# Listing the third chunk's output ahead of the fourth chunk's preparation, with an order edge behind it

## The chip, the cores and the metric

The kernel runs on one core of one Trainium2 chip. The metric is the device time of one execution in microseconds (us); lower is better. The engines are TensorE (PE in the profile, with PEld for its weight loads), VectorE (DVE), ScalarE (ACT), GpSimd (POOL) and SyncE (SP), which issues most of the DMA transfers.

## The reference, cut to what matters

Three layers follow each other, all in float32:

```python
# 1. linear attention with decay: batch 4, 8 heads, 768 steps, head size 48
for t in range(S):
    state = alpha[:, :, t, :, None] * state + einsum('bhd,bhe->bhde', k[:, :, t], v[:, :, t])
    y[:, :, t] = einsum('bhd,bhde->bhe', q[:, :, t], state)
# 2. dense layer over 3072 tokens, 384 -> 2048 -> 384
h = x @ w_in;  x = (h * cos(h)) @ w_out
# 3. routed experts: 8 experts, 384 -> 1024 -> 384, one expert for each token
#    with x @ w_skip > 0; the other tokens pass unchanged
out[t] = x[t] + gate[t] * (relu(x[t] @ w1[e]) @ w2[e])
```

## The kernel before, in words

**Chunks and groups.** The 3072 tokens are cut into 24 chunks of 128 steps. They are worked on in the order given by ORDER: the first chunks of three of the batches come first (indices 0, 1 and 2), then the rest; index 3 is the second chunk of the first batch. Three chunks make a group, and a group is the 384 columns that the dense layer takes at once. So the dense layer can start once the chunks 0, 1 and 2 have all delivered their columns. In this document the first chunk is index 0, the third is index 2, the fourth is index 3 and the fifth index 4.

**One chunk.** `prep(n, j)` has six parts, written p*nj* in the opening list: p*n*0 is the check of the decay's maximum (nothing for the first six chunks, whose check is `lim` on ScalarE), p*n*1 the first scan on VectorE (L401, and for the fourth chunk `lim` behind it: L378 and L380 on ScalarE), p*n*2 small operations for the seed of the second scan (L408, L411, L413), p*n*3 the second scan (L415), p*n*4 the product of q and k with the decays (L424; for the chunks 0 to 2 half of it is on GpSimd, L421), p*n*5 copies of k on ScalarE (L389), preceded for the fourth chunk by a scaling of a state on VectorE (L520). Then come T (transposes of k, L435 and L437), S0 and S1 (scores, L444 and the masked copy L445), Y0 and Y1 (the output in PSUM, L454 to L460) and U (the state, L500 and L511 to L514). a*n* is `lim` of a chunk on its own.

**The split of the output.** Y1 ends with the split of the output into a high part, rounded to the matmul's format (a copy on ScalarE), and a low part, the rest (a subtraction on VectorE), written to the tile X of the group. The first 96 rows go in one step, L480 and L481. The last 32 rows need another place: for most chunks through a small tile x3 (L475, L476) and DMAs (`s_late`, L491). For the third chunk, the only one in DIRECT, they are written to X straight from PSUM in three steps (L471 on ScalarE and L472 on VectorE, one pair for each of three blocks), and `s_late` issues nothing. Y*n*0 and Y*n*1 are called in the list as Y20 and Y21 for the third chunk.

**The weights.** w_in and w_out are stored as 64-bit numbers and come in 32 pieces. `piece64` is a generator with a step for each part of a piece: load (SP, L67), two copies on ScalarE (L76, L77), two operations on VectorE (L79, L82; the result is one of four buffers, YB), the high part on ScalarE (L309) and the low part on GpSimd (L310); a piece of w_out also goes through TensorE for the gate columns (L316 to L327). Five load buffers are used in turn (SB64). In the opening list, each g*i* is one step of the generator i; the pieces 0, 1 and 3 are of w_in, 2 and 4 of w_out.

**The dense layer.** For a slice f of 128 hidden columns `m_L1` is nine matmuls (L541), then L544 on ScalarE and L545 on VectorE; `m_mid` is the sine (L552, ScalarE) and a product (L553, VectorE); `m_split` is a copy (L560, ScalarE) and a subtraction (L562, GpSimd); `m_L2` is nine matmuls (L576). A group has 16 slices, and slice f needs piece f of both weights.

**What sets the order.** PRE is the opening list, written by hand; it is traced before the main loop's slots t = 0, 1, and so on. While it is traced, SP and GpSimd keep the written order (`manual_schedule`). TensorE, VectorE and ScalarE have a planner: it takes, by its own model of durations, the ready instruction that was traced first, so an instruction that is listed later can be issued earlier where the earlier one isn't ready. Steps that aren't in the list (the later weight pieces, the fifth chunk) are traced in the main loop. Each engine then runs its instructions in the order that came out. Loads of rows (`a_load_w`, tag w, L359) have two buffers, those of q and k (L365) three; a load waits until all readers of its buffer are done.

Of the kernel before, what the change touches and what calls it, by code (L numbers as in the profile page):

```python
# [7 lines left out]
F32 = mybir.dt.float32  # L8
# [5 lines left out]
ACTF = mybir.ActivationFunctionType  # L14
ALU = mybir.AluOpType
AX = mybir.AxisListType

B, H, S, D = 4, 8, 768, 48
# [22 lines left out]

PRE = """
w1 w0 p01 q2 q1 p11 q0 c g1 v0 w2 v1 g0 g2 g3 p02 p03 g4 p04 p12
T0 q3 mk g0 v2 p05 w3 p00 S00 p10 p20 p21 a0 a2 S01 Y00 p13 p14 Y01 p22 U0 p23 p24 p15 S10 S11 g0 g0 Y10 g2 p25 p30 g1 T1 p31 L0 U1 Y11 g1 S20 T2 S21 p32 p33 L1 Y20 g2 Y21 g3 p34 L2 g3 a1 U2 p35 g2 g3 g1
""".split()
LASTV = 1
RB = 2
# [181 lines left out]
def linear_attention_moe_kernel(outer, tc, qk, al, v, w_in, w_out, w1, w2, idw, cst, csti, fill, q0, k0, v0, alpha0, out):  # L229
    nc = tc.nc  # L230
# [144 lines left out]
    def lim(n):  # L375
        wA = raw[n][:, 8 * RL:16 * RL]
        junk = w64.tile([PR, 8 * RL], U8, tag="sq", name="sq", bufs=1)
        nc.scalar.activation(out=junk, in_=wA, func=ACTF.Relu, bias=lims[0:PR, 0:1], accum_out=amax[:, n:n + 1])  # L378
        i = NCH + LIM_ACT.index(n)
        nc.scalar.activation(out=junk, in_=wA, func=ACTF.Relu, scale=-1.0, bias=lims[0:PR, 1:2], accum_out=amax[:, i:i + 1])  # L380
# [49 lines left out]
    def s_T(n):  # L430
        if n not in NEXT:
            return
        pt = ps.tile([P, 512], F32, tag="t", name="pt")
        for p in range(NP):
            nc.tensor.transpose(pt[:, PR * p:PR * p + PR], QK[n][:, 1, p, :], ident[0:PR, 0:PR])  # L435
        t = at.tile([P, NP, PR], F32, tag="kT", name="kT", bufs=1)
        nc.scalar.activation(out=t.rearrange("p a b -> p (a b)"), in_=pt[:, 0:NP * PR], func=ACTF.Copy)  # L437
        kT[n] = t

    def s_S(n, i):  # L440
        N = 128 - 64 * i
        sc = ps.tile([P, 512], F32, tag="acc0" if i and n < 3 else "s", name="sc")[:, 0:NP * N].rearrange("p (a b) -> p a b", b=N)
        for p in range(NP):
            nc.tensor.matmul(sc[:, p, :], KB[:, 1 - i, p, :], QK[n][:, 0, p, 64 * i:128], start=True, stop=True)  # L444
        nc.vector.copy_predicated(out=scm[i], mask=mask[:, :, 0:N], data=sc)  # L445

    def s_Y(n, i):
        if i == 0:
            YP[n] = ps.tile([P, NP, 128], F32, tag="y", name="y")
        y = YP[n]  # L450
        first = FIRST[n]
        for p in (3, 0) if i == 0 else (1, 2):
            if not first:
                nc.tensor.matmul(  # L454
                    y[0:96, p, :], state(n)[:, p, :], QK[n][:, 0, p, :], start=True, stop=False, skip_group_check=True
                )
            nc.tensor.matmul(  # L457
                y[0:96, p, :], Vt[n][:, 1, p, :], scm[0][:, p, :], start=first, stop=False, skip_group_check=True
            )
            nc.tensor.matmul(  # L460
                y[0:96, p, 64:128], Vt[n][:, 2, p, :], scm[1][:, p, :], start=False, stop=True, skip_group_check=True
            )
        if i == 1:
            g, c = grp_of[n]
            if c == 0:
                X[g] = mo.tile([P, 2, 3, 128 * len(GROUPS[g])], F32R, tag="x", name="x")
            sl = slice(128 * c, 128 * c + 128)
            if n in DIRECT:
                for j in range(3):
                    hi, lo, yj = X[g][96:128, 0, j, sl], X[g][96:128, 1, j, sl], y[32 * j:32 * j + 32, 3, :]  # L470
                    nc.scalar.activation(out=hi, in_=yj, func=ACTF.Copy)  # L471
                    nc.vector.tensor_tensor(out=lo, in0=yj, in1=hi.bitcast(F32), op=ALU.subtract)  # L472
            x3 = n not in DIRECT and at.tile([96, 2, 128], F32R, tag="x3", name="x3")
            if x3:
                nc.scalar.activation(out=x3[:, 0, :], in_=y[0:96, 3, :], func=ACTF.Copy)  # L475
                nc.vector.tensor_tensor(  # L476
                    out=x3[:, 1, :], in0=y[0:96, 3, :], in1=x3[:, 0, :].bitcast(F32), op=ALU.subtract
                )
            hi, lo = X[g][0:96, 0, :, sl], X[g][0:96, 1, :, sl]
            nc.scalar.activation(out=hi, in_=y[0:96, 0:3, :], func=ACTF.Copy)  # L480
            nc.vector.tensor_tensor(out=lo, in0=y[0:96, 0:3, :], in1=hi.bitcast(F32), op=ALU.subtract)  # L481
            late[n] = x3


    def s_late(n):
# [9 lines left out]
    def s_U(n):  # L495
        if n not in NEXT:
            return
        u = ps.tile([P, 512], F32, tag="acc1" if n < 3 else "t", name="u")[:, 0:8 * D].rearrange("p (a b) -> p a b", b=2 * D)
        for p in range(NP):
            nc.tensor.matmul(u[0:PR, p, :], kT[n][:, p, :], Vt[n][:, 0, p, :], start=True, stop=True)  # L500
        if NEXT[n] == n + 1:
            Dc = at.tile([PR, NP], F32, tag="Dc", name="Dc")
            nc.vector.tensor_tensor(out=Dc, in0=TT[n][:, 0, :], in1=TT[n + 1][:, 1, :], op=ALU.mult)
        else:
            Dc = TT[n][:, 0, :]
        for a, b in ((0, 0), (64, D)):
            mb = state(n)[a:a + D, :, b:b + D]
            uv = u[a:a + D, :, b:b + D]
            db = Dc[a:a + D, :].rearrange("p (a b) -> p a b", b=1).to_broadcast([D, NP, D])
            if FIRST[n]:  # L510
                nc.vector.tensor_tensor(out=mb, in0=uv, in1=db, op=ALU.mult)  # L511
            else:
                nc.vector.tensor_tensor(out=mb, in0=uv, in1=mb, op=ALU.add)
                nc.vector.tensor_tensor(out=mb, in0=mb, in1=db, op=ALU.mult)  # L514
# [7 lines left out]
    def attn_step(n, j):  # L522
        if j == 0:
            s_T(n)
        elif j in (1, 2):
            s_S(n, j - 1)
        elif j in (3, 4):
            s_Y(n, j - 3)
        else:
            s_U(n)  # L530

# [122 lines left out]
    with ExitStack() as order_ctx:  # L654
# [21 lines left out]
        def consts():  # L676
            nc.sync.dma_start(out=cst_sb, in_=cst[:, 0:296])
            nc.sync.dma_start(out=idw_sb, in_=idw)
# [18 lines left out]
        for g, cs in enumerate(GROUPS):  # L697
            if g == 0:
                slots = list(range(-6 * len(cs), 0))
            else:  # L700
                free = list(range(32 * (g - 1), 32 * g - 4))
                k = 6 * len(cs)
                slots = [free[i * len(free) // k] for i in range(k)]
            for c, n in enumerate(cs):
                my = slots[6 * c:6 * c + 6]
                start[n] = my[0]
                for j, t in enumerate(my):
                    on(t, 1, attn_step, n, j)
                    if j == 4:
                        on(t + 3 if g else min(t + 3, -1), 3, s_late, n)  # L710
# [42 lines left out]

        def once(fn, *args):
            done[fn, args] = done.get((fn, args), 0) + 1
            fn(*args)

        def mk():
            nc.gpsimd.memset(run, 0.0)
            nc.gpsimd.tensor_copy(slot0, ebase)  # L760
            nc.vector.tensor_copy(mask, cst_sb[:, 168:296].rearrange("p (o s) -> p o s", o=1).to_broadcast([P, 4, 128]))
            nc.vector.tensor_copy(ustrict, cst_sb[:, 0:128])

        assert all(n in LIM_ACT or PRE.index(f"p{n}0") < PRE.index(f"p{n}1") for n in range(4))
        for c in PRE:
            k, a = c[0], c[1:]
            if c == "mk":
                mk()
            elif c == "c":
                consts()  # L770
            elif k == "a":
                lim(int(a))
            elif k == "g":
                once(next, gens[int(a)], None)
            elif k == "p":
                once(prep, int(a[:-1]), int(a[-1]))
            elif k in "TU":
                once(attn_step, int(a), 0 if k == "T" else 5)
            elif k in "SY":
                once(attn_step, int(a[:-1]), int(a[-1]) + (1 if k == "S" else 3))  # L780
            elif k == "L":
                once(s_late, int(a))
            else:
                once(dict(w=a_load_w, q=a_load_qr, v=a_load_v)[k], int(a))
        early = []
        for t in sorted(ev):
            if t <= 40:
# [21 lines left out]
        for t in range(0, END + 2 * LAG + 1):  # L809
# [36 lines left out]
        n = len(GROUPS[g])  # L846
        rs = mo.tile([P, 2, n, DM], F32R, tag="x", name="rs")
        split_row = lambda c: nc.vector.tensor_tensor(
            out=rs[:, 1, c, :], in0=acc[g][c][:, 0:DM], in1=rs[:, 0, c, :].bitcast(F32), op=ALU.subtract
# [29 lines left out]
        for c in range(n):  # L879
            sel.append(mo.tile([P, 128 * n], F32R, tag="gh", name="sel", bufs=LAG + 1)[:, 0:CAP])  # L880
            nc.vector.tensor_scalar(
                out=sel[c], in0=slot_ids, scalar1=pos_t[g][:, c, :], scalar2=None, op0=ALU.is_equal
# [236 lines left out]
```

## Time and profile before

| | before |
|---|---|
| median of 3 runs | 805.01 us (802.08 to 810.82) |
| the profiled execution | 804.26 us |
| its span, first to last instruction | 802.3 us |
| mean granted TensorE clock | 0.963 |
| TensorE busy | 750.4 us (94%) |
| VectorE busy | 520.3 us (65%) |
| ScalarE busy | 419.1 us (52%) |
| GpSimd busy | 246.4 us (31%) |

The span is that of the profiled execution; its own time is 1.96 us longer. Busy shares are means over stages with different limits. Matmuls overlap in the trace's rows, so a row of two can be longer than the time in which the next one may start.

### The profile page before, as it was taken

To read this page: it belongs to the slowest core of one execution; us is meant where nothing else is said; L and a number is where in the kernel's file an instruction comes from. 1 tells how busy PE (TensorE), PEld (TensorE's weight loads), DVE (VectorE), ACT (ScalarE), POOL (GpSimd) and SP (SyncE) were. 2 spreads that over 40 slices of the span, in tenths; PEclk is the share of its full clock that TensorE was granted. 3 is DMA by queue.
4 is the path that set the end of the run, shared out by engine and by line. 5 is a ranking of instruction groups with operands and counts; after the bars stand their busy time and mean duration, and the time that the engine had idled before them with its cause. 6 is when DMAs were issued, how large, how long until landed. Compare 5 with 4: busy or idle time off the path is not lost.

```text
span 802.3 us, 13591 instructions
## 1 busy us (share of the span) xinstructions
PE 750.4 (94%) x5033; PEld 732.9 (91%) x5033; DVE 520.3 (65%) x1080; ACT 419.1 (52%) x877; POOL 246.4 (31%) x249
## 2 busy tenths in 40 slices
PE   6788897999999999999999999999999879999995
PEld 4777796999999999999999999999998879999994
DVE  5899797866667666765756654444445457777772
ACT  3687785454454445435445444545555345555551
POOL 3165565324223332422423322232342011111112
PEclk8888989799999999999999999999999989999998
DMA  9766564233213313323332221202022656666631
GB/s 274 220 215 206 178 223 144 92 111 97 82 54 88 90 59 111 97 82 102 90 94 71 58 66 52 65 21 85 30 76 79 159 152 190 201 192 186 195 117 26
DMA packets 55121, 94.90 MB, mean 118 GB/s; under 512 B 7742, under 2 KB 41265, under 8 KB 55048
## 3 DMA queue, kind: packets, MB, share of 16 engines
q1 hardware_dynamic: 49432, 88.96, 36.6%
q0 software_dynamic: 4992, 4.80, 2.0%
q8 instruction: 41, 0.67, 0.4%
q14 instruction: 32, 0.26, 0.1%
q10 hardware_dynamic: 624, 0.21, 0.1%
HBM read 82.17 MB, written 16.43 MB: 123 GB/s over the span
## 4 chain that ended last, share of the span: by engine, by line
PE 59%; issue 17%; DMA 8%; DVE 6%; POOL 4%; ACT 3%; POOLq 1%; SPq 0%; ACTq 0%; DVEq 0%
PE acc L576 23%; PE h L541 23%; PE sc L444 5%; DMA qk<-qk 4%; POOL out L990 3%; DMA w<-al 2%; PE y L457 2%; PE y L454 2%; DMA xg<-xs 2%; PE u L500 2%; PE y L460 1%; DVE w L401 1%; DVE qk L424 1%; PE pt L435 1%; DMA v<-v 1%
## 5 line engine op out<-in xcount | busy, mean ns | idle before, releaser
L562 POOL TENSOR_TENSOR gl<-n,gh 128x384 fp32r<-128x384 f32 x127 | 135.4, 1067 | 301.0 <-ACT gh L560 236.8
L541 PE MATMUL h<-x,win_h 128*128 128x384 f32 x768 | 208.2, 352 | 7.2 <-ACT x L480 5.5
L541 PEld LDWEIGHTS h<-x,win_h 128*128 128x128 f32 x768 | 139.7, 193 | 9.3 <-ACT x L480 5.7
L576 PE MATMUL acc<-wout_h,gh 128*128 128x394 f32 x384 | 137.5, 358 | 0.0
L552 ACT ACTIVATE n<-n,lims 128x384 f32<-128x384 f32 x128 | 78.9, 616 | 109.7 <-DVE n L545 107.0
L576 PE MATMUL acc<-wout_h,gl 128*128 128x394 f32 x384 | 132.5, 345 | 0.3 <-POOL gl L562 0.3
L541 PE MATMUL h<-x,win_l 128*128 128x384 f32 x384 | 132.6, 345 | 0.0
L576 PE MATMUL acc<-wout_l,gh 128*128 128x394 f32 x384 | 132.4, 345 | 0.0
L545 DVE SCALAR_TENSOR_TENSOR n<-n,h 128x384 f32<-128x384 int32 x128 | 70.3, 549 | 83.3 <-ACT n L544 82.8
L560 ACT ACTIVATE gh<-n 128x384 fp32r<-128x384 f32 x128 | 66.9, 523 | 74.3 <-DVE n L553 73.4
L553 DVE TENSOR_TENSOR n<-n,h 128x384 f32<-128x384 f32 x128 | 70.5, 551 | 52.2 <-ACT n L552 50.9
L954 PE MATMUL h<-xt,w1t 128*128 128x276 f32 x576 | 89.0, 299 | 5.0 <-ACT xt L866 4.3
L544 ACT ACTIVATE n<-h 128x384 int32<-128x384 f32 x128 | 62.0, 485 | 52.9 <-PE h L541 47.1
L971 PE MATMUL acc<-ha,w2t 128*128 128x276 f32 x384 | 84.2, 292 | 0.0
L954 PEld LDWEIGHTS h<-xt,w1t 128*128 128x128 f32 x576 | 77.7, 190 | 6.2 <-ACT xt L866 4.6
L541 PEld LDWEIGHTS h<-x,win_l 128*128 128x128 f32 x384 | 74.2, 193 | 0.0
L576 PEld LDWEIGHTS acc<-wout_h,gl 128*128 128x128 f32 x384 | 73.1, 190 | 0.6 <-POOL gl L562 0.6
L576 PEld LDWEIGHTS acc<-wout_h,gh 128*128 128x128 f32 x384 | 73.6, 192 | 0.0
L576 PEld LDWEIGHTS acc<-wout_l,gh 128*128 128x128 f32 x384 | 73.4, 191 | 0.0
L990 POOL DMA_INDIRECT out<-res,xg x24 | 28.2, 1177 | 145.5 <-DVE res L987 143.2
L971 PEld LDWEIGHTS acc<-ha,w2t 128*128 128x128 f32 x384 | 65.1, 190 | 0.0
L957 ACT ACTIVATE ha<-h 128x276 fp32r<-128x276 f32 x64 | 25.6, 399 | 59.4 <-PE h L954 58.2
(149 smaller groups left out, 1273.2 us busy)
## 6 DMA issues: line engine op xcount, KB each, us to landing
st<-w SPq DMA_DIRECT2D x64, 384.0 KB
v<-v SPq DMA_DIRECT2D x24, 576.0 KB
qk<-qk SPq DMA_DIRECT2D x24, 448.0 KB
w<-al SPq DMA_DIRECT2D x22, 462.0 KB
st<-w_in SPq DMA_DIRECT2D x16, 384.0 KB
st<-w_out SPq DMA_DIRECT2D x16, 384.0 KB
out<-R SPq DMA_DIRECT2D x6, 576.0 KB
xs<-fill SPq DMA_DIRECT2D x8, 424.8 KB
```

What stands on the lines that cost most here:

```text
L444: nc.tensor.matmul(sc[:, p, :], KB[:, 1 - i, p, :], QK[n][:, 0, p, 64 * i:128], start=True, stop=True)
L541: nc.tensor.matmul(h, a[:, k, fs], X[g][:, i, k, :], start=(n == 0), stop=(n == 8))
L544: nc.scalar.activation(out=n, in_=h, func=ACTF.Copy, scale=1.0 / TWO_PI, bias=0.25)
L545: nc.vector.scalar_tensor_tensor(out=u, in0=n, scalar=-TWO_PI, in1=h, op0=ALU.mult, op1=ALU.add)
L552: nc.scalar.activation(out=u, in_=u, func=ACTF.Sin, bias=quarter)
L553: nc.vector.tensor_tensor(out=u, in0=u, in1=h, op=ALU.mult)
L560: nc.scalar.activation(out=a, in_=u, func=ACTF.Copy)
L562: eng.tensor_tensor(out=b, in0=u, in1=a.bitcast(F32), op=ALU.subtract)
L576: nc.tensor.matmul(acc[g][j][:, 0:WC], x[:, js], w[:, f, :], start=(f == 0 and i == 0), stop=(f == NF - 1 and i == 2))
L954: nc.tensor.matmul(h, w[:, i, k, fs], x[:, k, :], start=(n == 0), stop=(n == 8))
L971: nc.tensor.matmul(ACC[e][j], w[:, wi, f, js], x, start=(f == 0 and i == 0), stop=(f == NF2 - 1 and i == 2))
L990: ins = nc.gpsimd.indirect_dma_start(out=out[:, :], out_offset=bass.IndirectOffsetOnAxis(ap=x[:, j, RW - 1:RW].bitcast(I32), axis=0), in_= ...
```

## The change

The opening list is reordered: p30 to p33 (the fourth chunk's preparation up to its second scan) move from their places between p25 and Y20 to behind Y21, and a1 (the check of limits of the second chunk) moves ahead of them; the order of all other entries stays. `s_Y` returns the two instructions L480 and L481, and `once` and `attn_step` hand them on. When Y21 has been traced, `tc.issue_after` is entered for both: each instruction traced from there to the end of the list on ScalarE is ordered behind the third chunk's L480, and each on VectorE behind its L481. It is an order on the same engine, with no semaphore of its own. Instructions traced later, in the main loop, get no such edge.

```diff
 PRE = """
 w1 w0 p01 q2 q1 p11 q0 c g1 v0 w2 v1 g0 g2 g3 p02 p03 g4 p04 p12
-T0 q3 mk g0 v2 p05 w3 p00 S00 p10 p20 p21 a0 a2 S01 Y00 p13 p14 Y01 p22 U0 p23 p24 p15 S10 S11 g0 g0 Y10 g2 p25 p30 g1 T1 p31 L0 U1 Y11 g1 S20 T2 S21 p32 p33 L1 Y20 g2 Y21 g3 p34 L2 g3 a1 U2 p35 g2 g3 g1
+T0 q3 mk g0 v2 p05 w3 p00 S00 p10 p20 p21 a0 a2 S01 Y00 p13 p14 Y01 p22 U0 p23 p24 p15 S10 S11 g0 g0 Y10 g2 p25 g1 T1 L0 U1 Y11 g1 S20 T2 S21 L1 Y20 g2 Y21 a1 p30 p31 p32 p33 g3 p34 L2 g3 U2 p35 g2 g3 g1
 """.split()
...
-            nc.scalar.activation(out=hi, in_=y[0:96, 0:3, :], func=ACTF.Copy)
-            nc.vector.tensor_tensor(out=lo, in0=y[0:96, 0:3, :], in1=hi.bitcast(F32), op=ALU.subtract)
+            a = nc.scalar.activation(out=hi, in_=y[0:96, 0:3, :], func=ACTF.Copy)
+            b = nc.vector.tensor_tensor(out=lo, in0=y[0:96, 0:3, :], in1=hi.bitcast(F32), op=ALU.subtract)
             late[n] = x3
+            return a, b
...
+        behind = ExitStack()
         for c in PRE:
...
             elif k in "SY":
-                once(attn_step, int(a[:-1]), int(a[-1]) + (1 if k == "S" else 3))
+                last = once(attn_step, int(a[:-1]), int(a[-1]) + (1 if k == "S" else 3))
+                if c == "Y21":
+                    for i in last:
+                        behind.enter_context(tc.issue_after(i.ins))
...
+        behind.close()
```

## Rows read from the trace of the kernel before

**Rows 1.** The page, its first part: busy us, share of the span, instructions.
```profile
PE 750.4 (94%) x5033; PEld 732.9 (91%) x5033; DVE 520.3 (65%) x1080; ACT 419.1 (52%) x877; POOL 246.4 (31%) x249
```
**Rows 2.** Busy by stretch: PE, PEld, DVE, ACT, POOL, clock, DMA share, GB/s.
```profile
50.00:90.00 40.00, 35.68 (x228) 33.14 (x227) 39.53 (x70) 31.34 (x81) 26.02 (x23) 0.91 0.64 197
...
150.00:190.00 40.00, 40.00 (x264) 39.91 (x264) 26.94 (x63) 19.85 (x41) 11.01 (x14) 0.96 0.20 60
```
**Rows 3.** ScalarE in order of time: start, us, line, operation, idle before.
```profile
34.28 0.55 ACT L77 ACTIVATE st<-st 128x384 uint32<-128x384 uint32 x1 [1.46 <-issue]
...
37.06 0.27 ACT L471 ACTIVATE x<-y 32x128 fp32r<-32x128 f32 x1 [1.41 <-PE y L460]
...
37.35 0.55 ACT L76 ACTIVATE st<-st 128x384 f32<-128x384 f32 x1
...
37.81 0.72 ACT L378 ACTIVATE sq<-w,lims 112x528 uint8<-112x528 f32 x1
...
38.64 0.27 ACT L471 ACTIVATE x<-y 32x128 fp32r<-32x128 f32 x1
...
40.08 0.72 ACT L378 ACTIVATE sq<-w,lims 112x528 uint8<-112x528 f32 x1
...
40.92 0.27 ACT L471 ACTIVATE x<-y 32x128 fp32r<-32x128 f32 x1
...
42.68 0.49 ACT L480 ACTIVATE x<-y 96x384 fp32r<-96x384 f32 x1 [0.64 <-DVE x L472]
```
**Rows 4.** VectorE in order of time.
```profile
34.86 0.56 DVE L79 SCALAR_TENSOR_TENSOR y<-st 128x384 uint32<-128x384 uint32 x1 [1.30 <-ACT st L77]
...
35.34 2.10 DVE L401 TENSOR_TENSOR_SCAN w<-w,runA 112x528 f32<-112x528 f32 x1
...
37.46 0.28 DVE L472 TENSOR_TENSOR x<-y,x 32x128 fp32r<-32x128 f32 x1
...
40.08 0.28 DVE L472 TENSOR_TENSOR x<-y,x 32x128 fp32r<-32x128 f32 x1
...
40.40 1.93 DVE L424 TENSOR_TENSOR qk<-qk,w 112x1024 f32<-112x1024 f32 x1
...
42.36 0.29 DVE L472 TENSOR_TENSOR x<-y,x 32x128 fp32r<-32x128 f32 x1
...
43.81 0.55 DVE L481 TENSOR_TENSOR x<-y,x 96x384 fp32r<-96x384 f32 x1
...
44.98 0.56 DVE L79 SCALAR_TENSOR_TENSOR y<-st 128x384 uint32<-128x384 uint32 x1 [0.62 <-issue]
...
45.57 0.56 DVE L82 SCALAR_TENSOR_TENSOR y<-st,y 128x384 uint32<-128x384 uint32 x1
...
46.75 1.25 DVE L401 TENSOR_TENSOR_SCAN w<-w,runA 112x528 f32<-112x528 f32 x1
...
69.12 1.21 DVE L424 TENSOR_TENSOR qk<-qk,w 112x1024 f32<-112x1024 f32 x1
```
**Rows 5.** TensorE in order of time, the first and the second matrix.
```profile
43.22 1.01 PE L541 MATMUL h<-x,win_h 128*128 128x384 f32 x2 [5.50 <-ACT x L480]
...
49.03 0.42 PE L541 MATMUL h<-x,win_h 128*128 128x384 f32 x1
```
**Rows 6.** GpSimd in order of time.
```profile
35.32 1.00 POOL L310 TENSOR_TENSOR wout_l<-y,wout_h 128x384 fp32r<-128x384 f32 x1 [4.83 <-ACT wout_h L309]
...
40.25 2.93 POOL L310 TENSOR_TENSOR win_l<-y,win_h 128x384 fp32r<-128x384 f32 x2 [3.93 <-ACT win_h L309]
```
**Rows 7.** Waits, 37 to 200 us and SP's own: us, times, longest.
```profile
DVE qk L424 <- DMA qk<-qk: 5.9, 2, 4.5
...
DVE amax L398 <- DMA w<-al: 5.2, 2, 4.0
...
SPq L67 <- DVE y L82: 57.0, 23, 6.2
```
**Rows 8.** SP's queue of DMA issues in order of time.
```profile
42.39 0.33 SPq L359 DMA_DIRECT2D w<-al  x1
```

More of the change, by code (lines that the diff above doesn't have):

```diff
@@ L527, in attn_step @@
         elif j in (3, 4):
-            s_Y(n, j - 3)
+            return s_Y(n, j - 3)
         else:
@@ L755, in once @@
             done[fn, args] = done.get((fn, args), 0) + 1
-            fn(*args)
+            return fn(*args)
         def mk():
```

## The prediction, made before the changed kernel was run

> **What bounds the kernel now.** I read the page's first part, then the busy time by stretch, then the opening in order of time on each engine. The page shows TensorE busy for 750.4 of 802.3 us [rows 1], so a change can only pay in the 52 us in which it is not. The stretches show where those lie. Ahead of the first matrix stands one wait of 5.50 us, taken up below; from 50 to 90 TensorE works 35.68 of 40, while VectorE works 39.53 of those 40; from 150 to 190 TensorE works all 40.00 [rows 2]. So the opening is a dependence chain, the stretch behind it belongs to VectorE, and everything after belongs to TensorE. The change acts on the chain; what that is worth is decided in the stretch behind it.
>
> The chain is the third chunk's output. Its three DIRECT copies on ScalarE (L471) start at 37.06, 38.64 and 40.92, the wide copy (L480) at 42.68 [rows 3]; between them stand three subtractions on VectorE (L472) at 37.46, 40.08 and 42.36, and the wide one (L481) at 43.81 [rows 4]. The two engines take turns: each start of one follows the end of the other's, unless the engine is busy with something else. And it is: L378 at 37.81 and 40.08 fills ScalarE [rows 3], the scan L401, the product L424 and smaller steps fill VectorE [rows 4]. All of these belong to the fourth chunk or to the check of limits. TensorE starts the first matrix (L541, weight piece 0) at 43.22 after 5.50 us of waiting for L480 [rows 5].
>
> **What the change removes.** With both engines free the turn is 0.27 (L471) + 0.29 (L472), and a hand-over costs 0.03 (L472 from 42.36 to 42.65, L480 at 42.68) [rows 3, 4]. Three turns and six hand-overs are 3 x 0.56 + 6 x 0.03 = 1.86, so L480 could start at 37.06 + 1.86 = 38.9 instead of 42.68: 3.8 us at most. The edges keep back only what is listed behind Y21. Steps of later weight pieces, traced after the list, may still slip between: L76 at 37.35 is one (0.55) [rows 3]. I allow 0.6 for one such operation and take L480 at 39.5, L481 right behind it at 40.0 (L480 lasts 0.49) and ended at 40.5 (0.55), and TensorE's start 0.54 behind L480, as now, at 40.0: **3.2 us sooner**. L481 now starts 0.64 after L480's end (43.17 to 43.81); that goes too, 3.8 in all for the end of the first matrix.
>
> **What the change moves.** Nothing is computed less. What VectorE did ahead of L481 is done behind it. From L79 at 34.86 to L481 at 43.81 VectorE had no visible pause: 8.95 us, less three L472 (0.87), is 8.1 us of moved work [rows 4]: the fourth chunk's scans and product, the third's state update, and the conversion of the fourth weight piece (g3, also listed behind Y21). Two operations in it are longer than their like: L401 2.10 against 1.25 at 46.75, L424 1.93 against 1.21 at 69.12 [rows 4]. Without these 1.57 us it is 6.5. I take the middle, 7.3.
>
> So VectorE ends the moved work at 40.5 + 7.3 = 47.8, and only then goes on where it now goes on at 44.98: **2.8 us later**, if it stands idle meanwhile. Against that stands what can fill the hole. From 34.86 to 40.0 are 5.1 us, less 0.87 for L472: room of 4.2. The fifth weight piece was already being prepared at 37.35 [rows 3], and one piece takes VectorE 0.56 + 0.55 = 1.1 (L79 at 44.98, L82 at 45.57) [rows 4]. One piece leaves 1.7, two leave 0.6; a third I exclude, since two of the four buffers of converted pieces stay held until ScalarE's and GpSimd's steps behind Y21. I take half way, **1.1 us later**. Ends: no slip, 6.5 moved and two pieces filled, 39.9 + 6.5 - 44.98 - 2.2 = -0.8; no fill and 0.85 lost three times (the port, below), 40.5 + 6.5 + 2.55 - 44.98 = +4.6.
>
> ScalarE is treated alike. It now idles 1.46, 1.41 and 0.64 ahead of L77, L471 and L480 [rows 3], 3.5 us. With the edges it has only three L471 (0.8) and two pieces (2.2 at 0.55 an operation) between about 32.8 and 39.5: 3.7 idle. That is nothing to set beside VectorE's loss, and I add nothing.
>
> The limits of chunk 2 (a1) move ahead of the fourth chunk's preparation: same instructions, no cost, but they let go of a row buffer sooner. p30 issues nothing (the fourth chunk's limits are on ScalarE). SP's and GpSimd's written order stays as it was; what changes there is when their semaphores come. DMAs: none is added. GpSimd's subtractions for three pieces (L310, 1.00 and 2.93 for two) [rows 6] come behind ScalarE's copies, which are now behind L480. The second matrix needs one of them. By the terms above the fourth piece's VectorE steps end by about 45, its ScalarE copy by 45.5, and the two GpSimd operations by 48.5; TensorE now takes the second matrix at 49.03 [rows 5], so this stays covered with half a microsecond to spare; what GpSimd is late beyond that, TensorE would lose.
>
> **Why 3.2 us sooner is not the result.** From 50 to 90 VectorE has 0.47 us free in 40 [rows 2]. A matrix that comes sooner brings its two VectorE operations sooner, but each must still share the engine with the same conversions, and a hidden slice cannot pass the conversion of its own weights. At its end that stretch meets waits for DMA: 4.0 us on a row load (L398) and 4.5 on a q/k load (L424). Their issues stand in SP's queue among weight loads, which wait for VectorE's L82 23 times, 57.0 us in sum [rows 7], so they move with VectorE, not with TensorE. The sum: 804.26 of the profiled execution (span 802.30 and 1.96 around it) + 1.1 = **805.4**. The three runs shown have their median at 805.01, 0.75 above the profiled one, and reach from 802.08 to 810.82.
>
> **Rivals.** *The head start is kept.* If the stretch behind is in truth held by the ScalarE-GpSimd-TensorE turn through each slice, the 3.8 us stay: 804.26 - 3.8 = 800.5, or 799.9 without a slip. For it: TensorE and ScalarE both have waits left in 50 to 90. Against it: VectorE's 39.53 of 40. Chance 0.22.
>
> *The row load comes late (slower).* Place: SP issues a load of rows for the fifth chunk at 42.39, which the trace releases by L424, ended at 42.33 [rows 4, 8]. With the moved work L424 may end as late as 47.8, so the load leaves 5.5 later. Now it has landed by 46.75, when the fifth chunk's scan starts; then by 52.2 at latest. VectorE reaches that scan at 46.75 + 1.1 = 47.9 and, taking its work in order, would stand up to 4.3 us: 805.4 + 4.3 = 809.7. It decides once L424 ends more than about 1 us after its present 42.33. Against it: a1, now ahead, frees the other row buffer at about 42, and the load may be given that one. Chance 0.15.
>
> *The port.* L401 at 35.34 ran beside GpSimd's L310 at 35.32 and lost 0.85; L424 at 40.40 ran beside the pair at 40.25 and lost 0.72 [rows 4, 6]. If each of the three GpSimd pieces, all pushed behind L480, now meets a VectorE operation with two inputs, the moved work is 6.5 + 3 x 0.85 = 9.05 instead of 7.3: 807.2. Chance 0.10. The Trainium skill (SBUF — State Buffer, "SBUF: two separate sides") states as a rule that GpSimd and a two-input VectorE operation hold a shared port by an exclusive lock and that the later one waits in full; by that rule the loss could reach a whole GpSimd operation each time. The trace agrees with a loss, of 0.85 and 0.72 beside operations of about 1.00.
>
> *It does not do what it says.* Other pieces fill the freed turns, L480 stays near 42, and the time at 804 to 805. Chance 0.08. That leaves 0.45 for the forecast.
>
> **How the numbers follow.** The likeliest case is 805.4, its own ends 804.26 - 0.8 = 803.5 and 804.26 + 4.6 = 808.9. The range takes in the kept head start (799.9) and the late load (809.7), and some of the spread of the three runs above it: 799.5 to 811. A measurement of this kernel tells about 1%, 8 us, from no change. No single case goes so far. Faster by that much needs the kept 3.8 and one of the two DMA waits gone as well, 0.08; slower needs the late load and a longer DMA wait behind it, 0.10; within 1%, 0.82.
>
> **What would show it.** Right: L480 starts between 38.9 and 40, the first matrix by 40.5; the fourth chunk's first scan starts right behind L481; VectorE idles 2 to 4 us between 33 and 40; the scan of the fifth chunk starts 0.5 to 3 us later than 46.75; and the DMA wait at L398 is reached no sooner than now. Wrong: a TensorE that has done more slices by 90 us (then the head start was kept), or VectorE idle ahead of the fifth chunk's scan (then the row load was late).

## The result, and the profile after

The changed kernel takes 811.34 us (median of 20 runs, 806.02 to 816.13) against 806.14 us for the kernel before (20 runs beside them, 801.52 to 811.33): a ratio of 1.0054, 95% interval 1.0030 to 1.0079. The means, 811.14 and 806.75, lie 4.4 us apart, and this document uses that figure; the medians lie 5.2 apart. The change is inside the 1% that the prediction called no change, yet the interval shows that the kernel is slower. The profiled execution took 809.43 us, span 807.6, mean granted clock 0.955.

The rows that answer to those of before, in the same order. The changed kernel has one line more from L483 on, so L541, L545 and L552 of before are L542, L546 and L553 here. The page's first part [rows 1]:

```profile
PE 757.2 (94%) x5033; PEld 739.8 (92%) x5033; DVE 519.9 (64%) x1080; ACT 418.6 (52%) x877; POOL 250.3 (31%) x249
```
Busy by stretch [rows 2]: VectorE, 39.53 busy before from 50 to 90, now has 2.3 us free there, and TensorE spends about the same busy time on 199 matmuls where it had done 228, at a mean clock of 0.80 (before 0.91).

```profile
50.00:90.00 40.00, 35.96 (x199) 33.95 (x199) 37.73 (x66) 29.27 (x77) 25.84 (x22) 0.80 0.60 187
...
150.00:190.00 40.00, 40.00 (x258) 39.67 (x257) 28.38 (x65) 19.42 (x40) 11.55 (x13) 0.94 0.20 62
```
ScalarE in order of time [rows 3]. The split ends with L480 at 37.65, 5.0 us sooner than 42.68. The last steps of pieces 2 and 1 (L309), at 34.73 and 35.15 before, now come behind it:

```profile
34.36 0.26 ACT L471 ACTIVATE x<-y 32x128 fp32r<-32x128 f32 x1 [0.25 <-PE y L460]
...
37.65 0.49 ACT L480 ACTIVATE x<-y 96x384 fp32r<-96x384 f32 x1
...
41.09 0.51 ACT L309 ACTIVATE wout_h<-y 128x384 fp32r<-128x384 f32 x1
...
42.23 0.51 ACT L309 ACTIVATE win_h<-y 128x384 fp32r<-128x384 f32 x1
...
54.69 0.60 ACT L553 ACTIVATE n<-n,lims 128x384 f32<-128x384 f32 x1
```
VectorE [rows 4]. Four waits for ScalarE, 2.24 + 1.20 + 0.67 + 0.79 = 4.9 us, and nothing between them but the split. The fourth chunk's scan follows L481 at once, the fourth piece (L82 at 43.88, 38.00 before) behind it, and the fifth chunk's scan starts 5.7 us later than before (52.42 against 46.75):

```profile
34.65 0.28 DVE L472 TENSOR_TENSOR x<-y,x 32x128 fp32r<-32x128 f32 x1 [2.24 <-ACT x L471]
36.14 0.29 DVE L472 TENSOR_TENSOR x<-y,x 32x128 fp32r<-32x128 f32 x1 [1.20 <-ACT x L471]
37.10 0.29 DVE L472 TENSOR_TENSOR x<-y,x 32x128 fp32r<-32x128 f32 x1 [0.67 <-ACT x L471]
38.17 0.55 DVE L481 TENSOR_TENSOR x<-y,x 96x384 fp32r<-96x384 f32 x1 [0.79 <-ACT x L480]
38.65 1.24 DVE L401 TENSOR_TENSOR_SCAN w<-w,runA 112x528 f32<-112x528 f32 x1
...
42.75 1.21 DVE L424 TENSOR_TENSOR qk<-qk,w 112x1024 f32<-112x1024 f32 x1
43.88 0.54 DVE L82 SCALAR_TENSOR_TENSOR y<-st,y 128x384 uint32<-128x384 uint32 x1
44.46 1.04 DVE L521 TENSOR_TENSOR M<-M,T_all 48x192 f32<-48x192 f32 x1
45.53 0.55 DVE L546 SCALAR_TENSOR_TENSOR n<-n,h 128x384 f32<-128x384 int32 x1
...
52.42 1.25 DVE L401 TENSOR_TENSOR_SCAN w<-w,runA 112x528 f32<-112x528 f32 x1
```
TensorE [rows 5] takes the first matrix 5.0 us sooner, and the second in pieces: its high weights at 42.79, its low weights only at 48.21, which is where it took the whole second matrix before (49.03):

```profile
38.19 1.28 PE L542 MATMUL h<-x,win_h 128*128 128x384 f32 x2 [2.65 <-ACT x L480]
...
42.79 0.61 PE L542 MATMUL h<-x,win_h 128*128 128x384 f32 x2 [1.08 <-ACT win_h L309]
...
48.21 0.69 PE L542 MATMUL h<-x,win_l 128*128 128x384 f32 x1 [0.15 <-POOL win_l L310]
```
GpSimd [rows 6] keeps the written order of the list, g2 g3 g1: the low half of piece 1, the second of the pair at 45.88, stands behind that of piece 3.

```profile
41.68 3.60 POOL L310 TENSOR_TENSOR wout_l<-y,wout_h 128x384 fp32r<-128x384 f32 x1 [5.05 <-ACT wout_h L309]
45.88 2.28 POOL L310 TENSOR_TENSOR win_l<-y,win_h 128x384 fp32r<-128x384 f32 x2 [0.60 <-ACT win_h L309]
```
The first L310 lasts 3.60 beside the scan L415, the conversion L79 and the product L424, against 1.00 at 51.08. The Trainium skill (SBUF — State Buffer, "SBUF: two separate sides") states that the loser of the port that GpSimd shares with VectorE blocks fully. The loss of 2.6 us agrees with a block; it is longer than any one of the VectorE operations beside it (1.24 at most), so it spans several of them in a row.

Waits from 37 to 200 us [rows 7]: the DMA waits remain, somewhat shorter. SP [rows 8]: the fifth chunk's row load leaves at 40.04, sooner than 42.39; a later one, that of the eighth chunk, leaves at 95.36.

```profile
DVE qk L424 <- DMA qk<-qk: 4.0, 2, 3.0
...
DVE amax L398 <- DMA w<-al: 3.3, 2, 3.2
```
```profile
40.04 0.33 SPq L359 DMA_DIRECT2D w<-al  x1
...
94.98 0.33 SPq L67 DMA_DIRECT2D st<-w_in  x1
95.36 0.42 SPq L359 DMA_DIRECT2D w<-al  x1
```
In the kernel before that load left at 88.61, ahead of two weight loads that now stand in front of it:

```profile
88.61 0.34 SPq L359 DMA_DIRECT2D w<-al  x1
89.78 0.34 SPq L67 DMA_DIRECT2D st<-w_out  x1
91.20 0.33 SPq L67 DMA_DIRECT2D st<-w_in  x1
```
VectorE meets it. First before, then after, VectorE's check (L398) and product (L424) of the eighth chunk: 6.5 and 12.4 us later.

```profile
96.73 0.70 DVE L398 TENSOR_REDUCE amax<-w 112x1 f32<-112x528 f32 x1 [4.00 <-DMA w<-al]
...
106.84 1.92 DVE L424 TENSOR_TENSOR qk<-qk,w 112x1024 f32<-112x1024 f32 x1
```
```profile
103.24 0.70 DVE L398 TENSOR_REDUCE amax<-w 112x1 f32<-112x528 f32 x1 [3.19 <-DMA w<-al]
...
119.21 1.88 DVE L424 TENSOR_TENSOR qk<-qk,w 112x1024 f32<-112x1024 f32 x1
```

**Where the time went.** The 128 sines of the dense layer are the milestones. Both kernels were profiled twice (the second profiles are e12 and e8, below). Starts in us:

| | first matrix | 1st sine | 14th | 21st | 29th | 128th | span |
|---|---|---|---|---|---|---|---|
| before, two profiles | 43.22, 41.67 | 53.97, 54.28 | 140.74, 140.97 | 175.57, 176.62 | 209.75, 211.00 | 609.23, 611.63 | 802.3, 805.9 |
| after, two profiles | 38.19, 39.25 | 54.69, 55.79 | 143.33, 144.97 | 177.58, 176.95 | 213.93, 212.66 | 614.21, 615.57 | 807.6, 808.5 |
| difference of the means | -3.7 | +1.1 | +3.3 | +1.2 | +2.9 | +4.5 | +4.0 |

The first matrix is 3.7 us sooner, and nothing is left of that at the first sine. In the first pair of profiles most of it is still there one step ahead of the sine: VectorE's L546 starts at 45.53, 4.0 us sooner than L545 before (49.51). Its result is there at 46.08, but the sine starts only at 54.69: in ScalarE's order steps of later weight pieces and a copy (L437) stand in front of it. Before, the same distance was 3.9 us:

```profile
49.51 0.54 DVE L545 SCALAR_TENSOR_TENSOR n<-n,h 128x384 f32<-128x384 int32 x1
...
53.97 0.61 ACT L552 ACTIVATE n<-n,lims 128x384 f32<-128x384 f32 x1
```
By the 14th sine the kernel is clearly behind. The difference of the spans, 4.0, is close to that of the means of the runs, 4.4.

### The profile page after: what moved, and what is told of

Its sections match the earlier page's. It is cut to its first block, busy times and chain, and to the rows that moved or that the text cites. A ratio compares the mean times of both kernels' runs of the same rounds, so it can differ in the third digit from the quotient of the medians.

```text
span 807.6 us, 13589 instructions
## 1 busy us (share of the span) xinstructions
PE 757.2 (94%) x5033; PEld 739.8 (92%) x5033; DVE 519.9 (64%) x1080; ACT 418.6 (52%) x877; POOL 250.3 (31%) x249
## 4 chain that ended last, share of the span: by engine, by line
PE 63%; issue 18%; DMA 7%; POOL 5%; DVE 3%; ACT 2%; POOLq 0%; SPq 0%; ACTq 0%; DVEq 0%
PE acc L577 24%; PE h L542 24%; PE sc L444 5%; DMA w<-al 4%; POOL out L996 3%; PE y L457 2%; PE y L454 2%; PE u L501 2%; DMA xg<-xs 2%; PE y L460 2%; PE wg L322 1%; POOL gl L563 1%; DMA qk<-qk 1%; PE pt L435 1%; DMA x<-x 1%
## 5 line engine op out<-in xcount | busy, mean ns | idle before, releaser
L563 POOL TENSOR_TENSOR gl<-n,gh 128x384 fp32r<-128x384 f32 x127 | 139.1, 1096 | 305.0 <-ACT gh L561 241.3
L542 PE MATMUL h<-x,win_h 128*128 128x384 f32 x768 | 210.8, 356 | 4.8 <-ACT x L480 2.7
L542 PEld LDWEIGHTS h<-x,win_h 128*128 128x128 f32 x768 | 142.4, 197 | 6.3 <-ACT x L480 2.7
L542 PE MATMUL h<-x,win_l 128*128 128x384 f32 x384 | 134.6, 351 | 0.2 <-POOL win_l L310 0.2
L553 ACT ACTIVATE n<-n,lims 128x384 f32<-128x384 f32 x128 | 78.8, 616 | 99.4 <-DVE n L546 97.9
L546 DVE SCALAR_TENSOR_TENSOR n<-n,h 128x384 f32<-128x384 int32 x128 | 70.2, 549 | 84.3 <-ACT n L545 83.9
L545 ACT ACTIVATE n<-h 128x384 int32<-128x384 f32 x128 | 62.0, 484 | 56.5 <-PE h L542 52.9
L542 PEld LDWEIGHTS h<-x,win_l 128*128 128x128 f32 x384 | 75.6, 197 | 0.4 <-POOL win_l L310 0.4
L444 PEld LDWEIGHTS sc<-qk,kb 112*128 112x128 f32 x384 | 51.4, 200 | 5.6 <-DVE runB L408 2.5
```

Of the source, the lines that this page charges most:

```text
L542: nc.tensor.matmul(h, a[:, k, fs], X[g][:, i, k, :], start=(n == 0), stop=(n == 8))
L545: nc.scalar.activation(out=n, in_=h, func=ACTF.Copy, scale=1.0 / TWO_PI, bias=0.25)
L546: nc.vector.scalar_tensor_tensor(out=u, in0=n, scalar=-TWO_PI, in1=h, op0=ALU.mult, op1=ALU.add)
L553: nc.scalar.activation(out=u, in_=u, func=ACTF.Sin, bias=quarter)
L563: eng.tensor_tensor(out=b, in0=u, in1=a.bitcast(F32), op=ALU.subtract)
```

## The experiments

**e1, the list alone** (no edges), **e2, the edges alone** (on the old list, so that pieces, p34 and a1 are held, but not p30 to p33), **e3, only the fourth chunk's scans held** (a1 and p30 to p33; the edges are closed at the first g3 behind Y21) and **e4, two last steps first** (the whole change, but pieces 2 and 1 end ahead of Y21).

```diff
# e1                                   # e2: PRE as before, edges as changed
-                if c == "Y21":
-                    for i in last:
-                        behind.enter_context(tc.issue_after(i.ins))
# e3
...
+            if c == "g3" and last is not None:
+                behind.close()
...
# e4
-... Y20 g2 Y21 a1 p30 p31 p32 p33 g3 p34 L2 g3 U2 p35 g2 g3 g1
+... Y20 g2 g2 g1 Y21 a1 p30 p31 p32 p33 g3 p34 L2 g3 U2 p35 g3
```
Expected:

> The reordered opening list with no order edge. Theory A (what is held back behind L480 and L481 costs more than the head start): without the edges the planner again fills the turns, L480 starts at 40 to 42, the work is not held back, and the time is within 0.2% of before (ratio 0.998 to 1.002). Theory B (the late part is an accident of the planner's new order, whatever the edge): ratio 1.003 to 1.008 as with the whole change.

> The old opening list with the order edges behind Y21: the fourth chunk's scans are free again, the three weight pieces' steps, p34, U2 and p35 are held behind L480 and L481. Theory A with the weight pieces as the costly part: the second matrix still waits for its low weights at about 48 and the ratio is 1.003 to 1.007. Theory A with the scans as the costly part: ratio 0.998 to 1.002. Theory B: ratio anywhere from 0.995 to 1.008 with no relation to the opening.

> The reordered list, with the edges on a1 and p30 to p33 alone: the weight pieces, p34, U2 and p35 are free. Theory A with the weight pieces as the costly part: the copies L309 of pieces 1 and 2 return to 34 to 36, the second matrix starts right behind the first, by 43, the first sine starts at 50 to 52 instead of 54.7, and the ratio is 0.995 to 1.000. Theory A with the scans: ratio 1.002 to 1.007.

> The whole change, but the last steps of weight pieces 2 and 1 (L309, L310) are listed ahead of Y21, so they are not held back. Theory A with the weight pieces: the second matrix no longer waits for L310, the opening's head start is kept into the second slice, the ratio is 0.995 to 1.001. Theory A with the scans, or B: ratio 1.003 to 1.007 as with the whole change.

Measured: e1 0.9999 (0.9978 to 1.0021), e2 0.9979 (0.9950 to 1.0009), e3 0.9970 (0.9944 to 0.9996), e4 0.9982 (0.9953 to 1.0010). No interval of the four overlaps that of the whole change, 1.0030 to 1.0079. e1 came as theory A said; e2 fell on the side of the scans, e3 and e4 on that of the pieces; e3's second matrix (45.65) and first sine (53.84) did not come as soon as expected. So neither the new list alone nor any of these partial holds costs the time. In e4 TensorE has the second matrix right behind the first (42.16, against 48.21 above), and the first sine starts at 47.2:

```profile
38.79 1.33 PE L542 MATMUL h<-x,win_h 128*128 128x384 f32 x3 [2.22 <-ACT x L480]
...
42.16 0.38 PE L542 MATMUL h<-x,win_h 128*128 128x384 f32 x1
```
On VectorE, e4 has the changed kernel's opening nearly row by row: four waits for ScalarE, 2.50 + 0.52 + 1.31 + 0.89 = 5.2 us, a late fourth piece (L82), and L546 at 45.44. Its fifth chunk's scan is later still (53.84). Yet it is not slower than the kernel before. **So the idle time in VectorE's opening and the late fourth piece do not by themselves cost the 4 us.** What differs is on ScalarE and GpSimd, which have done the last steps of pieces 2 and 1 ahead of the split; ScalarE comes to the first sine 7.5 us sooner:

```profile
35.20 0.28 DVE L472 TENSOR_TENSOR x<-y,x 32x128 fp32r<-32x128 f32 x1 [2.50 <-ACT x L471]
36.01 0.29 DVE L472 TENSOR_TENSOR x<-y,x 32x128 fp32r<-32x128 f32 x1 [0.52 <-ACT x L471]
37.60 0.29 DVE L472 TENSOR_TENSOR x<-y,x 32x128 fp32r<-32x128 f32 x1 [1.31 <-ACT x L471]
38.77 0.55 DVE L481 TENSOR_TENSOR x<-y,x 96x384 fp32r<-96x384 f32 x1 [0.89 <-ACT x L480]
...
44.48 0.54 DVE L82 SCALAR_TENSOR_TENSOR y<-st,y 128x384 uint32<-128x384 uint32 x1
...
45.44 0.55 DVE L546 SCALAR_TENSOR_TENSOR n<-n,h 128x384 f32<-128x384 int32 x1
...
47.20 0.60 ACT L553 ACTIVATE n<-n,lims 128x384 f32<-128x384 f32 x1
```
A late first sine is not enough either: in e2 it starts at 54.72 and, in a second profile (e11), at 55.84. In e3 the fourth piece fills VectorE's hole, ahead of the first L472:

```profile
35.02 0.56 DVE L79 SCALAR_TENSOR_TENSOR y<-st 128x384 uint32<-128x384 uint32 x1 [1.30 <-ACT st L77]
35.61 1.27 DVE L82 SCALAR_TENSOR_TENSOR y<-st,y 128x384 uint32<-128x384 uint32 x1
37.46 0.28 DVE L472 TENSOR_TENSOR x<-y,x 32x128 fp32r<-32x128 f32 x1 [0.58 <-ACT x L471]
```

**e5, only the pieces held**: the new list, but the edges are entered at the first g3, behind p33. It parts "the held pieces alone cost it" from "both together".

```diff
-                    for i in last:
-                        behind.enter_context(tc.issue_after(i.ins))
+                    held = last
...
+            if c == "g3" and held:
+                for i in held:
+                    behind.enter_context(tc.issue_after(i.ins))
+                held = None
```


> The complement of e3: the reordered list, a1 and p30 to p33 free, and the edges on what stands behind p33 (the steps of the weight pieces 1, 2 and 3, p34, U2, p35). Theory A2 (holding back the weight pieces is what costs): the second matrix waits for L310 until 47 or later, the first sine starts after 54, slice 13 is reached 2 to 3 us later than before, ratio 1.002 to 1.008. Rival A1 (holding back the scans costs): ratio 0.998 to 1.001. Rival C (what the time comes to is set by where TensorE's clock falls to 1.2 GHz later on, the opening being made good or not): the opening as in A2, but a ratio anywhere from 0.996 to 1.006, that goes with TensorE's busy time.

Measured 0.9979 (0.9948 to 1.0010), as e2, which also holds the pieces alone. The held pieces by themselves are not slower; here VectorE does the fourth chunk's second scan (35.77) in the hole. Of the kernels run, only those lose the time that have both the scans and the last steps of pieces 2 and 1 behind the split: the changed kernel, and e6 and e9 below.

**e6 and e7, TensorE kept busy later.** In the changed kernel TensorE waits 2.20 us at 204.03, and the granted clock is at its low level (1.2 GHz) from 205.7 to 209.1. e6 adds to the whole change 8 matmuls behind the first matrix and 34 (128x112) in the second group's eighth slice; e7 adds the same 34 to e3. e6 and e7 do not compute the reference's output: the 34 write into the PSUM tile that holds the sums of the second group's third chunk.

```diff
# behind m_L2 of the second group's eighth slice, e6 and e7 (the 8 of e6 are left out here)
+        for _ in range({(1, 7): 34}.get((g, f), 0)):
+            nc.tensor.matmul(acc[g][2][:, WC:506], ones, ustrict[:, 0:506 - WC],
+                             start=True, stop=True, skip_group_check=True)
```


> The whole change, with dummy matmuls on TensorE in two of its waits: 8 of 128x512 behind the first matrix (wait from 42.8), 34 of 128x112 into unused columns ahead of the score matmuls at 204.0 (wait of 2.20 us). The order on the other engines is that of the change. Theory C (clock): TensorE stays at 2.4 GHz behind 204, the slices 20 to 28 take 34.2 to 34.9 us as before instead of 36.35, TensorE's busy time without the dummies falls by 3 us or more, ratio 1.001 to 1.004. Rival (the wait itself or the order is what costs, not the clock): slices 20 to 28 stay at 36 or more, ratio 1.004 to 1.007.

> e3 (edges on a1 and p30 to p33 alone) with the same 34 dummy matmuls ahead of the score matmuls that wait 2.04 us at 195.8. Theory C: slices 20 to 28 fall from 36.33 to about 34.5, ratio 0.993 to 0.997. Rival: 36 stays, ratio 0.996 to 0.999.

Measured: e6 1.0033 (1.0005 to 1.0060), e7 0.9997 (0.9971 to 1.0023). In both, the wait near 204 and the low stretch there are gone (the clock of 190 to 230 is 1.00, after 0.96), and e6 is still slower than before, while e7 lies no lower than e3. e6's ratio lies where its expectation put it for the clock, and its slices 20 to 28 take 33.9 us, 36.35 in the changed kernel; e7's ratio is that of neither side. So the later drop of the clock is not what makes the changed kernel slow as a whole, but a part of it, up to some 2 us (1.0054 less 1.0033), isn't excluded.

**e8, e11, e12: second profiles** of the changed kernel, of e2 and of the kernel before, all unaltered.

> The changed kernel once more, unaltered, for a second profile. Theory C: the fall to 1.2 GHz behind the wait at 204 comes again and slices 20 to 28 take 36.0 to 36.6 us; if it is a chance of one execution: 34.2 to 35.

> The old list with the edges, unaltered, a second look. In its first profile the opening was as late as in the changed kernel at the 14th sine (143.2 against 143.3), but the 21st came at 173.3 against 177.6, and the stretch at the low clock from 143 to 153, which the kernel before and the changed kernel show, was not there. If that stretch belongs to the order of the work, it is missing again and the 21st sine comes 29 to 31 us behind the 14th. If it is chance, it may be there, and the distance is then 34 to 35.

> The kernel before, unaltered, a second look. If the low stretch at 143 to 153 belongs to the order of the work, it is there again and the 21st sine starts 34 to 35 us behind the 14th, as in the first profile (34.8); if it is chance, it may be missing and the distance 29 to 31. The low stretches ahead of 110 recur within 1.5 us of their places.

Measured: 810.37, 805.15 and 807.89 us. The opening of the changed kernel recurs, row by row, 1.06 us later (L480 at 38.71, the same four waits); its low stretch at 144.3 to 154.5 doesn't, the one near 205 does (203.5 to 206.9). In e2 the stretch at 143 is missing in both profiles and the 21st sine comes 30.1 us behind the 14th both times; in the kernel before it is there both times and the distance is 34.8 and 35.7. For these two it belongs to the order of the work, as the expectation put it; for the changed kernel it came once in two profiles. Of the earlier low stretches of the kernel before, two came back near their places (65.3 and 99.5), two ran together into one from 38.0 to 51.7, and one at 126.8 is new; the expectation of 1.5 us was met in part.

**e9, the two last steps right behind the split**: the whole change, pieces 2 and 1 still held, but first in the list behind Y21.

```diff
-... Y20 g2 Y21 a1 p30 p31 p32 p33 g3 p34 L2 g3 U2 p35 g2 g3 g1
+... Y20 g2 Y21 g2 g1 a1 p30 p31 p32 p33 g3 p34 L2 g3 U2 p35 g3
```


> The whole change with one difference: the last steps of weight pieces 2 and 1 (ScalarE's L309 and GpSimd's L310) stand first in the list behind Y21 and no longer last; they are still ordered behind L480. It separates two reasons for the late second matrix. Theory Q (queueing): what costs is not the hold itself but that the two steps come behind the held limit checks on ScalarE (L378, L380) and that GpSimd's L310 then runs beside the held scans. Then L309 starts within 1 us of L480's end, TensorE takes the low weights of the second matrix by 43 to 45 and not 10.0 us behind the first matrix's start, the 14th sine starts 3 us or more sooner than the changed kernel's 143.3, and the ratio is 0.995 to 1.000 as in the kernel that lists them ahead of Y21. Theory H (hold): being behind L480 at all costs the time, about 3 us too late for the fourth piece: ratio 1.003 to 1.007.

Measured 1.0073 (1.0043 to 1.0102). The edit did on TensorE what theory Q asked for: no wait shows from the first matrix's start at 39.04 to the end of the second, near 44. But the ratio is near theory H's, the 14th sine starts at 147.48, 4 us later than 143.33 instead of 3 sooner, and theory Q falls. **With the late second matrix, which the trace of the changed kernel shows so plainly, taken away, nothing is gained.** The edit has a price on VectorE: the freed GpSimd steps now run beside the small steps of the scans (L408 and L413 0.74 and 0.99, 0.22 and 0.16 in the changed kernel), and L424 and the fourth piece come later still (L424 at 44.98 against 42.75).

```profile
40.91 0.74 DVE L408 TENSOR_SCALAR runB<-w 112x4 f32<-112x4 f32 x2
41.55 0.99 DVE L413 COPY T_all<-w 112x8 f32<-112x8 f32 x1
...
44.98 1.23 DVE L424 TENSOR_TENSOR qk<-qk,w 112x1024 f32<-112x1024 f32 x1
46.12 0.55 DVE L79 SCALAR_TENSOR_TENSOR y<-st 128x384 uint32<-128x384 uint32 x1
46.70 0.55 DVE L546 SCALAR_TENSOR_TENSOR n<-n,h 128x384 f32<-128x384 int32 x1
47.17 0.55 DVE L82 SCALAR_TENSOR_TENSOR y<-st,y 128x384 uint32<-128x384 uint32 x1
```
**e10, e3 and e4 together.**

> The two best single releases together: the last steps of pieces 2 and 1 are listed ahead of Y21, and the edges are closed ahead of g3, so that only a1 and p30 to p33 are held. If the two releases remove the same loss, the ratio is that of either alone, 0.996 to 0.999. If they remove separate losses, it is 0.993 to 0.995. The first matrix starts by 42, the 14th sine by 137.5.

Measured 0.9957 (0.9934 to 0.9979), 802.35 us: faster than the kernel before by about 3.5 us, and the best of all. The intervals of e3 and e4 contain 0.9957, so that the two releases add up is not shown, nor which of the two gives the gain. Behind one wait of 2.23 us VectorE has work at each turn of the split, and the fifth chunk's scan keeps its place (46.44):

```profile
34.29 0.56 DVE L79 SCALAR_TENSOR_TENSOR y<-st 128x384 uint32<-128x384 uint32 x1 [2.23 <-ACT st L77]
34.88 0.28 DVE L472 TENSOR_TENSOR x<-y,x 32x128 fp32r<-32x128 f32 x1
35.19 0.93 DVE L82 SCALAR_TENSOR_TENSOR y<-st,y 128x384 uint32<-128x384 uint32 x1
36.15 0.29 DVE L472 TENSOR_TENSOR x<-y,x 32x128 fp32r<-32x128 f32 x1
...
46.44 1.25 DVE L401 TENSOR_TENSOR_SCAN w<-w,runA 112x528 f32<-112x528 f32 x1
```
The kernels side by side (ends and starts in us; two numbers are two profiles):

| kernel | held behind the split | ratio | fourth piece's L82 ends | 14th sine | 21st sine |
|---|---|---|---|---|---|
| before | nothing | 1 | 38.6, 37.3 | 140.7, 141.0 | 175.6, 176.6 |
| e1 | nothing | 0.9999 | 39.2 | 140.2 | 174.9 |
| e2 | pieces | 0.9979 | 44.9, 46.0 | 143.3, 143.9 | 173.3, 173.9 |
| e5 | pieces | 0.9979 | 42.7 | 141.2 | 172.3 |
| e3 | scans | 0.9970 | 36.9 | 137.4 | 169.4 |
| e4 | scans, fourth piece | 0.9982 | 45.0 | 137.0 | 169.9 |
| e10 | scans | 0.9957 | 36.1 | 136.0 | 169.0 |
| after | scans and all pieces | 1.0054 | 44.4, 45.5 | 143.3, 145.0 | 177.6, 177.0 |
| e9 | scans and all pieces | 1.0073 | 47.7 | 147.5 | 180.8 |

Over the nine, the ratio follows the start of the 21st sine with a correlation of 0.92, and 1 us there goes with 0.72 us of the time. So most of the result is decided ahead of the 21st sine.

**What these runs do not part.** The kernels differ in more than the opening. Compared instruction by instruction, the traces show the changed kernel, e6 and e9 in the same order on VectorE, ScalarE, GpSimd and SyncE from 57 to 204 us, and all three are slower. The kernel before and e1 have one order on VectorE, ScalarE and GpSimd from 66 us on, and they take the same time. e2, e3, e4, e5 and e10 have other orders up to about 157 us, and none is slower. So the planner's order behind the opening, which each edit changed along with the holds, is a rival for the 4 us; no run held it fixed. The clock is a second one: the mean granted clock from 30 to 140 us is 0.84 in the changed kernel (0.83 in its second profile), e6 and e9, and 0.86 to 0.92 in all the others. It may follow from the waits as well as cause time. What the experiments show is which edits cost the time, not yet by what path.

## Why the prediction was right, and where it was not

The forecast, no change that can be told, held: +4.4 us against +1.1, within 1%. That the split would come sooner and that this would not show in the time was right. By what path the kernel becomes slower was not foreseen, and the runs leave it open. The predicted 805.4 is 4.0 below the profiled 809.43, which lies in the range; the median of 811.34 lies 0.3 above its end.

- **The split, 3.2 us sooner.** It was 5.0 and 2.4 in the two pairs of profiles, 3.7 in the mean, near the forecast partly by luck. From the first L471 to L480 were 5.62 and 6.68 us before and 3.30 in both profiles after, more than the 2.46 of the text (1.86 and one slip of 0.6): steps of two pieces slipped in. The rest is the first L471 itself, which the bound of 3.8 took at 37.06 as given. It moved to 34.36 with L460, which releases it, but it stands at 34.46 in the second profile of the kernel before, so this part is not shown to be the change's.
- **VectorE's moved work, ended at 47.8.** It was done at 45.5 (L521, 44.46 + 1.04), 6.8 behind the end of L481 at 38.7. The middle of 7.3 us was a little too much: L401 and L424 lasted 1.24 and 1.21, and only L521 (1.04, against 0.35 in e4) lost to GpSimd. The port rival fell on VectorE's side; it was GpSimd that lost (3.60).
- **What fills the hole. This step failed.** "One piece leaves 1.7, two leave 0.6 ... I take half way, 1.1 us late": no piece came in. VectorE's waits from 30 to 45 us rose from 1.9 to 4.9 in sum. The one piece that was ready, the fourth, is the one that the edge holds; released, it fills the hole (e3, e10). VectorE went on behind the moved work at 45.5, only 0.5 later than 44.98: the unfilled 1.7 was made up by a split that ended 1.8 sooner than the text took it and by the smaller 6.8. That the sum came near is luck. And the hole is not shown to cost the 4 us, since e4 has it and is not slower. Of the 5.7 us by which the fifth chunk's scan is later, the 0.5 is one part; two more conversions put ahead of it are 2.2, L546 and L445, now ahead too, are 1.3, and two L79 that took 2.57 beside GpSimd's pair, where e4 has 1.02, are 1.5.
- **GpSimd's pair, covered with half a microsecond to spare.** The size was right: the pair ended at 48.2, against 48.5. The comparison was wrong: it was made with 49.03, where the second matrix stood before, though a head start brings that forward too. TensorE was past the first matrix at about 42 and used the low weights of piece 1 at 48.21. e9 takes this wait away, at a price on VectorE, and gains nothing.
- **Why 3.2 us sooner is not the result.** Right in the outcome: nothing of the head start is left at the first sine. The place is another: the conversions that VectorE must still do did not spend it at once, since L546 was 4.0 us sooner; it is gone in ScalarE's order, where the sine stands 8.6 us behind its operand. e2 has as late a sine and is not slower, so the late sine is not shown to be the cost.
- **The late row load (slower).** Right as a mechanism, at another place: not the fifth chunk's load (40.04, sooner than before), but the eighth's, which left 6.75 us later, behind two weight loads, which SP's queue issues as VectorE's L82 ends. That its lateness is a part of the 4 us is argued from the rows; no run took it away by itself, and e5, which shows the same late load (96.63), is not slower.
- **The head start kept (faster).** Not with this edit. e10, which hides the split's turns behind the fourth piece, is 3.5 us faster, near the 3.8 that this rival was priced at; that it is this head start which it keeps is not shown.
- **The shown signs.** The fourth chunk's scan did start right behind L481; L480 came at 37.65, before the 38.9 to 40 expected, and the fifth chunk's scan later than the 0.5 to 3 us. VectorE's idle of 4.9 was above the 2 to 4.

Open: how e2, as late as the changed kernel at the 14th sine, gains some 3 us on it by the 21st in both its profiles; whether the holds themselves or the planner's order behind them costs the 4 us; and how much of the last 1 to 2 us (29th sine to end) is the change's. After the 21st sine the kernels differ by up to 5 us in their single profiles, in no order that the edits explain.

## What to carry to other kernels

An order edge that pulls one chain forward also holds other work back, and where a planner fills the rest, it changes the order far behind the edge too. Here two holds together went with a loss of 4 us, and either alone with none. An idle time on an engine is not yet a cost (e4 has the same one and is not slower), and a plain wait on the busiest engine isn't either (e9 takes it away and gains nothing): take it away by itself before building on it. And before blaming the place of the edit, compare the order of the instructions behind it; kernels that shared that order here were slower or equal together.

## What the runs showed of the hardware

- One kernel's runs spread over more than the effect: 801.1 to 810.1 us in the 35 runs of the kernel before that were taken beside e1 to e4. They go with the mean granted TensorE clock, 0.954 to 0.970, with a correlation of -0.71: those with less of it are longer. A single profile of each kernel would have put the difference at 5.3 us or, with the second profiles, at 2.6.
- A wait of TensorE of like length was followed by the low level of the clock in one kernel and not in another: before the scores L444 near 200 us, 2.20 in the changed kernel (1.61 in its second profile) and 2.04 in e3 were, 2.03 in e4 was not.
- GpSimd's L310 took 1.00 us at 51.08 and 3.60 at 41.68, where VectorE had L415, L79, L424 and L82 beside it without a pause. At the same place it took 3.63 in the second profile and 3.62 in e6.
